# S1 x T1 of the down projection as seven half-size products, and the second block's attention in another order

## The chip, the cores and the metric

The kernel runs on one core of a Trainium2 chip. The metric is the device time in microseconds (us) of one execution. PE is TensorE, DVE is VectorE, ACT is ScalarE, POOL is GpSimd and SP is SyncE; PEld is PE's loading of weights.

## The reference

```python
# S = 2048 tokens, D = 1024, F = 3584, 32 heads of 32, window W = 8, dilation 2
xn = layernorm(x)
q, k, v = split(xn @ wqkv)
logits[s, w] = q[s] . k[s - 2 w] * scale      # -1e9 where s - 2 w < 0
s = (softmax(logits) weighted sum of v[s - 2 w]) @ wo
h = silu(xn @ w1) * (xn @ w3)
g = silu(h @ w2)
out = x + s * g
```

## The kernel before

The tokens are worked in two blocks of 1024 (`b` is 0 or 1), each of two chunks of 512 (chunks 0 to 3; c0 is the even one of a block). Every large product is a 2 x 2 product of halves, done as seven half products with sums of operands before and sums of results after (Strassen's method in Winograd's form). A block goes through these stages on PE: q, k and v (`qkv_pairs`), in block 1 then the output projection of chunk 1 (`wo`), fourteen steps of gate and up projection (`up_step`), the down projection (`mlp_down`), and `wo` of the even chunk. `wo` of chunk 3 comes last.

`mlp_down` multiplies the hidden rows h (2 row halves x 2 halves of F) with w2 (2 halves of F x 2 halves of D). Its seven products run in the order: `w(0,0)`, `w(1,0)`, S2 x T2, S1 x T1, S4 x `w(1,1)`, S3 x T3, h x T4. Each has four row groups `g` of 128 tokens, and each group 14 matmuls of 512 columns on one bank of PSUM. T1 to T4 are sums of w2 that the program keeps in `t_dram`. The S are written by DVE; S1 lies where the tokens' transposed x or its sums were (`s1v`). In the product S1 x T1 the bank `pe[g]` is filled, ACT copies it to SBUF (`dsp`), and S4 x `w(1,1)` goes on adding to the same bank, after which DVE adds (`dsb`). The product S3 x T3 ends in a DVE addition `dsa`, and T4 goes on adding to that bank.

`attention(c)` runs on DVE: the scores (`qk`, `qa`, `qb`, `qc` into the tile E), an exchange over partitions by 16 DMAs (L), the softmax (`z`, `tr`, `zd`, `exp`, `rec`, `pb`), 16 DMAs back into E, and the weighted sum of v (`pv`, `pa`) into `qo`. q, k and v of later chunks wait in DRAM (`park`, `put`, `get`); kT and vT hold one chunk.

The order on every queue is fixed when the program is built. PE runs in the order of the program. The other engines and the DMA queues SP and POOL run in the order that a planner (`Plan`) finds: it lays out all operations with costs of its own and takes, of those ready, the one with the earliest due time, which follows from PE's plan. `plan.soon` shifts due times by name, `plan.chains` fixes the order of named operations, and a `mark` on an operation is a cell that others can wait for. `r8` is a pool of six 8 KB buffers for weights and rows, `k2` one of eight 2 KB buffers, `mm` the eight banks of PSUM. `ln_turn` issues a DMA transpose from ACT's queue. The shared helpers have one line each: `mm` 322, `tt` 331, `cp` 336, `mm_half` 347, `silu` 353, `dma` 359, `ln_turn` 523.

Of the kernel before, what the change touches and what calls it, by code (L numbers as in the profile page):

```python
# [209 lines left out]
def kernel(  # L210
# [489 lines left out]
    def attention(c):  # L700
        u = c % 2
        J4 = [range(0, 4), range(4, 8)]
        r4 = lambda s: s.ap().rearrange("p (j n) -> p j n", j=4)
        if ("q", c) in park:
            get(c, "q")
        if ("k", c) in park:
            halo("k")
            get(c, "k", [("E", W - 1, 3, NR - 1)] if c % 2 else [])
        for w in range(W):
            o = HALO - DIL * w  # L710
            pr = []
# [11 lines left out]
            tt(f"qc{c}", add, lambda w=w: E[:, :, w, :], lambda p0=p0: r4(p0)[:, 0].rearrange("p (q n) -> p q n", n=P),  # L723
               lambda p0=p0: r4(p0)[:, 1].rearrange("p (q n) -> p q n", n=P),
               [p0], [("E", w, sq, r) for sq in range(4) for r in range(NR)], 512, True)
        if ("v", c) in park:
            halo("v")
            get(c, "v")
        L = [plan.slot("att", f"L{c}_{i}") for i in range(2)]
        Lv = lambda i: L[i].ap().rearrange("p (r w n) -> p r w n", r=2, w=W)  # L730
        for r in range(NR):
            for sq in range(4):
                dma((POOL, SP)[sq % 2], f"L{c}", lambda r=r, sq=sq: Lv(r // 2)[sq * 32:(sq + 1) * 32, r % 2],
                    lambda r=r, sq=sq: E[r:P:NR, sq], [("E", w, sq, r) for w in range(W)], [(L[r // 2], r % 2, sq)], 117)
        zf = lambda s: s.ap().bitcast(FP32)
        z = plan.slot("att", f"z{c}")
        zv = lambda: zf(z).rearrange("p (w n) -> p w n", w=W)
        LC = [[(L[i], r, sq) for sq in range(4)] for i in range(2) for r in range(2)]
        tt(f"z{c}", add, zv, lambda: Lv(0)[:, 0], lambda: Lv(0)[:, 1], LC[0] + LC[1], [z], 1024, False)
        tt(f"z{c}", add, zv, zv, lambda: Lv(1)[:, 0], LC[2] + [z], [z], 1024, False)  # L740
        tt(f"z{c}", add, zv, zv, lambda: Lv(1)[:, 1], LC[3] + [z], [z], 1024, False)
        if c == 0:
            tt(f"z{c}", add, lambda: zv()[:, :, 0:HALO], lambda: zv()[:, :, 0:HALO], lambda: maskb[:], [z], [z], 128, False)
        zm = plan.slot("att", f"zm{c}")
        zt = lambda s: zf(s)[:, 0:512].rearrange("p (w n) -> p w n", w=4)

        def tree(t, op):
            tt(f"tr{c}", op, lambda: zt(t), lambda: zv()[:, 0:4], lambda: zv()[:, 4:8], [z], [t], 512, False)
            tt(f"tr{c}", op, lambda: zt(t)[:, 0:2], lambda: zt(t)[:, 0:2], lambda: zt(t)[:, 2:4], [t], [t], 256, False)
            tt(f"tr{c}", op, lambda: zt(t)[:, 0:1], lambda: zt(t)[:, 0:1], lambda: zt(t)[:, 1:2], [t], [t], 128, False)  # L750

        tree(zm, mx)
        tt(f"zd{c}", sub, zv, zv, lambda: zt(zm)[:, 0:1].to_broadcast([P, W, P]), [z, zm], [z], 1024, False)
        plan.op(ACT, f"exp{c}", lambda: nc.scalar.activation(out=zf(z), in_=zf(z), func=ACTF.Exp, scale=scale),  # L754
                [z], [z], 1.07, 0.11, table="exp")
        zs = plan.slot("att", f"zs{c}")
        tree(zs, add)
        plan.op(DVE, f"rec{c}", lambda: nc.vector.reciprocal(out=zt(zs)[:, 0], in_=zt(zs)[:, 0]), [zs], [zs], 0.87)
        pb = plan.slot("att", f"pb{c}")
        pbv = lambda: pb.ap()[:, 0:1024].rearrange("p (w n) -> p w n", w=W)  # L760
        tt(f"pb{c}", mul, pbv, zv, lambda: zt(zs)[:, 0:1].to_broadcast([P, W, P]), [z, zs], [pb], 1024, False)
        for r in range(NR):
            for sq in range(4):
                dma((POOL, SP)[sq % 2], f"E{c}", lambda r=r, sq=sq: E[r:P:NR, sq],
                    lambda sq=sq: pbv()[sq * 32:(sq + 1) * 32], [pb], [("E", w, sq, r) for w in range(W)], 117)
        for jh in range(2):
            js = slice(jh * 4, jh * 4 + 4)
            A = lambda js=js: qo[:, u, js, :]
            Ac = qo_cells(u, J4[jh])

            def pv(dst, wr, w, jh=jh, js=js):
                o = HALO - DIL * w
                q4 = lambda a: a.rearrange("p j (q n) -> p j q n", n=P)
                tt(f"pv{c}", mul, lambda: q4(dst()), lambda: E[:, :, w, :].unsqueeze(1).to_broadcast([P, 4, NST, P]),
                   lambda: q4(vT[:, js, o:o + CH]),
                   [("E", w, sq, r) for sq in range(4) for r in range(NR)] + [("v", j) for j in J4[jh]]
                   + ([("v", j, "halo") for j in J4[jh]] if w else []), wr, 2048, True)
# [170 lines left out]
    def mlp_down(b):  # L948
# [5 lines left out]
        def rhs_load(kind, fh=0, dh=0, t=0):  # L954
            res = []
            for q in range(FH // NQ):
# [3 lines left out]
                if kind == "t":  # L960
                    dma(SP, "t2", v, lambda q=q: t_dram[:, q * NQ:(q + 1) * NQ, t, :],
                        [("td", i) for i in range(q * NQ, (q + 1) * NQ)], [wt], 896)
# [33 lines left out]

        hb = lambda fh, row, g: (lambda: h_sb[:, F_[fh], gs[row][g]])
# [19 lines left out]
        for g in G:  # L1017
            tt("s1", add, lambda g=g: s1v(g), fit(g, hb(0, 1, g)), fit(g, hb(1, 1, g)), hcl(0, 1, g) + hcl(1, 1, g), s1_cells(g), NS, True)
            tt("s3", sub, hf(0, 1, g), hb(0, 0, g), hb(0, 1, g), hcl(0, 0, g) + hcl(0, 1, g), hcl(0, 1, g), NS, True)
        for g in G:  # L1020
            pb.append(bank(f"db{b}_{g}"))
            cp("dfork", pb[g].ap, pa[g].ap, [pa[g]], [pb[g]])
            tt("s2", sub, fit(g, hf(0, 0, g)), lambda g=g: s1v(g), fit(g, hb(0, 0, g)), s1_cells(g) + hcl(0, 0, g), hcl(0, 0, g), NS, True)
# [10 lines left out]
        for g in G:  # L1034
# [3 lines left out]
        rhs = rhs_load("t", t=T1)  # L1038
        pe, sp5 = [], []
        for g in G:  # L1040
            pe.append(bank(f"de{b}_{g}"))
            for q, (wt, ops) in enumerate(rhs):
                mm(pe[g], [lambda g=g, k=k: s1_k(g, k) for k in range(q * NQ, (q + 1) * NQ)], ops, q == 0,
                   [wt] + s1_cells(g), last=q == 1, mark=[("pr", 12 + g)])
            if b + 1 < NB and g == 0:
                ln_turn(2 * b + 3, 0, xn[1], ("pr", 12))
                ln_turn(2 * b + 3, 1, xn[1], ("pr", 12))
            if b + 1 < NB and g == 3:
                ln_turn(2 * b + 3, 2, xn[1], ("pr", 15))
                ln_turn(2 * b + 3, 3, xn[1], ("pr", 15))  # L1050
# [37 lines left out]
    def wo_load():  # L1088

        wots = []  # L1090
        for dh in range(2):
            wot = plan.slot("r8", f"wo{dh}")
            dma(SP, "wo", lambda wot=wot: wot.ap().rearrange("p (j n) -> p j n", j=NJ),
# [184 lines left out]
    plan.chains.append("qs5q0 qs5q1 qforkq0 qforkq1".split())  # L1278
    for st in range(NST):
# [20 lines left out]
    for b in range(NB):  # L1300
# [24 lines left out]
        else:  # L1325
            attention(c0 - 1)
# [18 lines left out]
        def first(b=b):  # L1345
            if b:
                w1o.extend(wo_load())
# [50 lines left out]
```

## Time and profile before

| | |
|---|---|
| median of 3 runs | 717.15 us (717.07 to 718.08) |
| profiled execution, span from first to last instruction | 715.3 us |
| the median less that span | 1.8 us |
| PE busy | 707.4 us |
| DVE busy | 643.8 us |
| ACT busy | 382.3 us |
| granted clock of PE | 1.000 |

The profile is one execution of its own; for it the span is given, and what lies around the span in a run is read as the difference to the median. Times within the profile count from the span's start. A line of the timeline or of a group names the start, the duration, the engine, the line of the program, the operation, what it writes and reads, and how many there were. Matmuls are pipelined, so the time from start to start is what one costs. Some records of matmuls are missing: a step of twice the usual length is such a one.

### The profile page before, as it was taken

Reading aid. Unit: us, or ns where it says so; the run is one execution under the profiler, and the core shown is the slowest. Engines: PE = TensorE matmul, PEld = TensorE weight load, DVE = VectorE, ACT = ScalarE, POOL = GpSimd, SP = SyncE. Lnnn points to the kernel's source line nnn. Section 1 sums busy time; section 2 is a strip of 40 time slices with the busy share of each in tenths; the row PEclk is TensorE's granted clock in tenths of the full one; section 3 lists DMA queues with packets and bytes.
Section 4 is the critical chain, followed back from the end, with each engine's and each line's share of the span. In section 5 each row is a group of like instructions: output and inputs, shape, how many; then the busy total and the mean of one; then the engine's idle time right before and its main releaser. Section 6 shows DMA issues by size and latency. Waiting matters only on the chain.

```text
span 715.3 us, 9199 instructions
## 1 busy us (share of the span) xinstructions
PE 707.4 (99%) x3287; PEld 343.0 (48%) x3342; DVE 643.8 (90%) x866; ACT 382.3 (53%) x650; POOL 50.7 (7%) x103
## 2 busy tenths in 40 slices
PE   9999999999999999999999999999999999999998
PEld 5555544444444444444555554444444444444443
DVE  7999999997999999599999999676999995899936
ACT  7644556575656799142545354676565654411133
POOL 1020100202000000202000000211000002200000
PEclk9999999999999999999999999999999999999999
DMA  9999966659644758994553569787537347655502
GB/s 331 290 358 345 350 224 203 222 155 300 207 148 169 258 181 237 212 269 125 174 170 131 180 198 337 261 283 244 173 129 239 114 153 213 214 191 177 177 21 97
DMA packets 132205, 151.34 MB, mean 212 GB/s; under 512 B 17216, under 2 KB 109248, under 8 KB 127808
## 3 DMA queue, kind: packets, MB, share of 16 engines
q1 hardware_dynamic: 117168, 121.98, 53.4%
q0 software_dynamic: 6112, 26.22, 10.2%
q10 hardware_dynamic: 8880, 2.56, 1.8%
q8 instruction: 26, 0.43, 0.2%
q14 instruction: 19, 0.16, 0.1%
HBM read 106.96 MB, written 32.51 MB: 195 GB/s over the span
## 4 chain that ended last, share of the span: by engine, by line
PE 99%; issue 0%; DVE 0%; ACT 0%; DVEq 0%
PE mm L322 97%; PE mm L307 1%; PE mm L501 0%; DVE xT L331 0%; ACT xT L508 0%; DVE r L435 0%; PE mm L347 0%; DVE k L305 0%; ACT small L424 0%; DVEq L1393 0%; DVE small L426 0%; DVE eps_t L290 0%; DVE eps_d L291 0%; DVEq L331 0%
## 5 line engine op out<-in xcount | busy, mean ns | idle before, releaser
L322 PEld LDWEIGHTS <-r 128*128 128x128 f16 (+1 forms) x2276 | 240.0, 107 | 244.5 <-DMA r<-in_A_wqkv_dram 0.5
L322 PE MATMUL mm<-xs,r 128*128 128x512 f16 x1280 | 295.2, 379 | 0.0
L322 PE MATMUL mm<-xT,r 128*128 128x512 bf16 (+2 forms) x956 | 224.3, 371 | 2.1
L336 ACT COPY k<-mm 128x512 f32<-128x512 f32 x192 | 112.4, 586 | 93.5 <-PE mm L322 93.0
L322 PE MATMUL mm<-r,h_sb 128*128 128x512 bf16 (+1 forms) x694 | 153.0, 379 | 0.5
L322 PEld LDWEIGHTS <-h_sb 128*128 128x128 f16 (+1 forms) x800 | 78.3, 98 | 94.4
L336 ACT COPY mm<-mm 128x512 f32<-128x512 f32 (+1 forms) x89 | 50.6, 571 | 72.2 <-PE mm L322 68.2
L331 DVE TENSOR_TENSOR a<-a,a 128x2048 bf16<-128x2048 bf16 (+1 forms) x72 | 87.7, 1218 | 0.3
L331 DVE TENSOR_TENSOR a<-qo,kT 128x2048 bf16<-128x2048 bf16 x64 | 77.4, 1219 | 1.4 <-ACT kT L336 1.3
L331 DVE TENSOR_TENSOR a<-E,vT 128x2048 bf16<-128x2048 bf16 x56 | 66.4, 1217 | 0.0
L331 DVE TENSOR_TENSOR k<-mm,k 128x512 f32<-128x512 f32 x72 | 48.1, 684 | 19.9 <-PE mm L322 19.8
L331 DVE TENSOR_TENSOR h_sb<-mm,k 128x512 bf16<-128x512 f32 x96 | 63.0, 684 | 1.0 <-PE mm L322 0.5
L353 ACT ACTIVATE k<-k 128x512 bf16<-128x512 f32 x56 | 34.9, 631 | 45.6 <-DVE k L331 45.6
L331 DVE TENSOR_TENSOR h_sb<-h_sb,k 128x1024 bf16<-128x1024 bf16 x56 | 37.1, 686 | 17.2 <-ACT k L336 17.2
L331 DVE TENSOR_TENSOR r<-r,r 128x1024 f16<-128x1024 f16 (+5 forms) x61 | 49.5, 818 | 0.9 <-DMA xT<-r 0.5
L353 ACT ACTIVATE h_sb<-mm 128x512 bf16<-128x512 f32 x60 | 35.8, 598 | 21.7 <-PE mm L322 21.6
L331 DVE TENSOR_TENSOR a<-a 128x1024 bf16<-128x1024 bf16 (+4 forms) x60 | 37.9, 633 | 6.8 <-ACT a L754 4.4
L336 ACT CAST k<-mm 128x512 bf16<-128x512 f32 x56 | 32.6, 585 | 12.2 <-PE mm L322 12.1
L331 DVE TENSOR_TENSOR qo<-qo,a 128x2048 bf16<-128x2048 bf16 x32 | 38.9, 1216 | 0.0
L359 POOL DMA_DIRECT2D a<-E x32 | 16.7, 528 | 303.6 <-ACT k L336 126.1
L331 DVE TENSOR_TENSOR h_sb<-h_sb 128x512 f16<-128x512 bf16 (+1 forms) x72 | 37.0, 575 | 0.0
L331 DVE TENSOR_TENSOR r<-r 128x1024 f16<-128x1024 bf16 (+1 forms) x34 | 25.7, 780 | 0.0
(98 smaller groups left out, 387.8 us busy)
## 6 DMA issues: line engine op xcount, KB each, us to landing
r<-in_B_w_dram SPq DMA_DIRECT2D x42, 512.0 KB, 4.3
s_dram<-r POOLq DMA_DIRECT2D x14, 1024.0 KB, 5.4
r<-t_dram SPq DMA_DIRECT2D x16, 896.0 KB, 6.1
r<-s_dram SPq DMA_DIRECT2D x14, 1024.0 KB, 4.8
r<-in_B_w_dram SPq DMA_DIRECT2D x12, 896.0 KB, 4.9
r<-in_A_wqkv_dram SPq DMA_DIRECT2D x10, 1024.0 KB, 7.3
h_sb<-in_B_w_dram SPq DMA_DIRECT2D x14, 512.0 KB, 8.9
t_dram<-h_sb POOLq DMA_DIRECT2D x14, 512.0 KB, 6.5
```

Source lines behind the costliest of these rows:

```text
L307: nc.tensor.matmul(plan.pools["mm"][i % 8][:], lhsT=warm[:, 0:P], rhs=warm[:, 0:CH], start=True, stop=True)
L322: nc.tensor.matmul(cut(ps.ap()), lhsT=lhs[k](), rhs=cut(rhs[k]()), start=(first and k == 0), stop=(last and k == n - 1), skip_group_check= ...
L331: plan.op(DVE, name, lambda: fn(out=o(), in0=a(), in1=b()), rd, wr, occ, 0.08, late=late)
L336: plan.op(ACT, name, lambda: nc.scalar.copy(out=o(), in_=a()), rd, wr, occ, 0.11)
L353: plan.op(ACT, name, lambda: nc.scalar.activation(out=o(), in_=a(), func=ACTF.Silu), rd, wr, occ, 0.11, table="silu")
L359: plan.op(eng, name, lambda: e.dma_start(out=o(), in_=a()), rd, wr, occ, 0.0, nbytes=kb * 1024, late=late)
```

## The change

S1 x T1 is done by `product2`. It splits S1 by row groups into two pairs and by F into even and odd hidden rows, and T1 by F in the same way and by columns into halves of 256, and multiplies by the same seven-product method once more: for each of two row groups, seven products of seven matmuls of 256 columns. Four sums of S quarters, four of T quarters and four additions on PSUM are new on DVE, copies of banks on ACT. One `r8` buffer (`ex`) holds two of the sums. T1 is loaded as even and odd rows. The last row group of S2 x T2 is placed behind the first two of the seven products. The transposes of chunk 3 wait for marks in the new product.

`attention` is cut into `scores`, `softmax` and `values`. For chunk 2 the softmax works in rows 20 to 27 of `h_sb`, and the result goes to an `r8` buffer instead of E, so that the scores of chunk 3 can be written to E meanwhile. In block 1 `scores` of chunk 2 stands before the up steps, `softmax` of chunk 2 and `scores` of chunk 3 before step 5, `values` of chunk 2 behind the steps. In block 0 `scores` of chunk 1 stands before `mlp_down`. Due times and one chain on SP are changed.

```diff
@@ attention(c), cut into scores, softmax, values @@
-    def attention(c):
+    def scores(c):
         u = c % 2
-        J4 = [range(0, 4), range(4, 8)]
-        r4 = lambda s: s.ap().rearrange("p (j n) -> p j n", j=4)
         if ("q", c) in park:
             get(c, "q")
         if ("k", c) in park:
             halo("k")
-            get(c, "k", [("E", W - 1, 3, NR - 1)] if c % 2 else [])
+            get(c, "k", [("E", W - 1, 3, NR - 1)] if c == 1 else [("L", 2)])
         for w in range(W):
...
+    def softmax(c):
+        if c != 2:
+            sl = [plan.slot("att", f"sm{c}_{i}") for i in range(3)]
+            L = [lambda i=i: sl[i].ap() for i in range(2)]
+            Lc = [lambda r, sq, i=i: (sl[i], r, sq) for i in range(2)]
+            z, zc = zf(lambda: sl[2].ap()), [sl[2]]
+            zmc, pbc = [sl[0]], [sl[1]]
+            zm, pb = zf(L[0]), lambda: sl[1].ap()[:, 0:1024]
+            Ec = "E"
+        else:
+            hi = plan.slot("r8", f"P{c}")
+            hrow = lambda f, n: h_sb[:, f:f + n, :].rearrange("p f n -> p (f n)")
+            hrc = lambda f, n: [x for k in range(f, f + n) for row in range(2) for x in h_cells([k], row)]
+            L = [lambda i=i: hrow(20 + 2 * i, 2) for i in range(2)]
+            Lc = [lambda r, sq, i=i: ("h", 20 + 2 * i + r, sq // 2, sq % 2) for i in range(2)]
+            z, zc = zf(lambda: hrow(24, 2)), hrc(24, 2)
+            zmc, pbc = hrc(26, 1), hrc(27, 1)
+            zm, pb = zf(lambda: hrow(26, 1)), lambda: hrow(27, 1)
+            Ec = hi
+        PB[c] = (Ec, (lambda: E[:]) if c != 2 else (lambda: hi.ap().rearrange("p (q w n) -> p q w n", q=NST, w=W)))
...
+                    [Lc[r // 2](r % 2, sq)] + [("L", c)] * ((r, sq) == (NR - 1, 3)), 117)
...
+                dma((POOL, SP)[sq % 2], f"E{c}", lambda r=r, sq=sq: P4()[r:P:NR, sq],
+                    lambda sq=sq: pbv()[sq * 32:(sq + 1) * 32], pbc,
+                    [(Ec, w, sq, r) for w in range(W)], 117)
+
+    def values(c):
+        u = c % 2
+        Ec, P4 = PB[c]
...
@@ mlp_down(b) @@
+                    fs = slice(q, FH, 2) if t == T1 else slice(q * NQ, (q + 1) * NQ)
+                    dma(SP, f"t2_{b}{t}{q}", v, lambda fs=fs: t_dram[:, fs, t, :],
+                        [("td", i) for i in range(FH)[fs]], [wt, (wt, 0), (wt, 1)], 896)
...
+        def product2(pe, rhs):
+            ex = plan.slot("r8", "ex")
+            HC = CH // 2
+            I = range(2)
+            w = [wt for wt, _ in rhs]
+            wv = lambda kk, n: (lambda: r8v(w[kk], FP16)[:, 0:NQ * CH].rearrange("p (k n) -> p k n", k=NQ)[:, :, n * HC:(n + 1) * HC])
+            tv = lambda: r8v(ex, FP16)[:, 0:NQ * HC].rearrange("p (k n) -> p k n", k=NQ)
+            uv = lambda: r8v(ex, FP16)[:, NQ * HC:2 * NQ * HC].rearrange("p (k n) -> p k n", k=NQ)
+            part = lambda m, kk, i: [("s1 part", 2 * m + i, kk)]
+            if b + 1 == NB:
+                rows = [((lambda m, kk: (lambda: s1_q2(m, kk))), uv, lambda m, kk: part(m, kk, 0) + part(m, kk, 1),
+                         [(ex, 1), (ex, 2)], 2 * NQ * P)]
+            else:
+                rows = [((lambda m, kk, i=i: (lambda: s1_q(2 * m + i, kk))), (lambda i=i: uv()[:, :, i * P:(i + 1) * P]),
+                         (lambda m, kk, i=i: part(m, kk, i)), [(ex, 1 + i)], NQ * P) for i in I]
+            def in_place(x, y, neg, n):
+                for r, (a, u, cells, uc, size) in enumerate(rows):
+                    dst, src = a(*x), u if y is None else a(*y)
+                    ry = uc if y is None else cells(*y)
+                    pair = (src, dst) if neg else (dst, src)
+                    tt(n, sub, dst, pair[0], pair[1], cells(*x) + ry, cells(*x), size, True)
+            for a, u, cells, uc, size in rows:
+                tt("l2s1", add, u, a(1, 0), a(1, 1), cells(1, 0) + cells(1, 1), uc, size, True)
+            in_place((1, 0), (0, 0), True, "l2s3")
+            tt("l2t1", sub, tv, wv(0, 1), wv(0, 0), [(w[0], 1), (w[0], 0)], [(ex, 0)], NQ * HC, True)
+            tt("l2t3", sub, wv(0, 1), wv(1, 1), wv(0, 1), [(w[1], 1), (w[0], 1)], [(w[0], 1)], NQ * HC, True)
+            lhs = lambda m, kk, i: ([lambda k=k: s1_q(2 * m + i, kk)[:, k, :] for k in range(NQ)],
+                                    part(m, kk, i) + s1_cells(2 * m + i))
+            lhu = lambda i: ([lambda k=k: uv()[:, k, i * P:(i + 1) * P] for k in range(NQ)], [(ex, 1 + i)])
+            rw = lambda kk, n: ([lambda k=k: wv(kk, n)()[:, k, :] for k in range(NQ)], [(w[kk], n), w[kk]])
+            rt = ([lambda k=k: tv()[:, k, :] for k in range(NQ)], [(ex, 0)])
+            def p(ps, n, A, B, first=False, mark=()):
+                a, ra = A
+                c, rc = B
+                def emit():
+                    for k in range(NQ):
+                        nc.tensor.matmul(half(ps.ap, n)(), lhsT=a[k](), rhs=c[k](), start=first and k == 0, stop=k == NQ - 1,
+                                         skip_group_check=True)
+                plan.op(PE, "mm2 " + ps.name, emit, ra + rc, [ps] + list(mark), NQ * 0.1092, 0.0)
+            for i in I:
+                p(pe[2 + i], 0, lhs(0, 0, i), rw(0, 0), True)
+            for i in I:
+                p(pe[2 + i], 1, lhu(i), rt)
+            in_place((0, 0), None, True, "l2s2")
+            tt("l2t2", sub, wv(0, 0), wv(1, 1), tv, [(w[1], 1), (ex, 0), (w[0], 0)], [(w[0], 0)], NQ * HC, True)
+            s15 = []
+            for i in I:
+                s15.append(plan.slot("k2", "l2s15"))
+                cp("l2s15", lambda i=i: f32(s15[i]), pe[2 + i].ap, [pe[2 + i]], [s15[i]])
+                cp("l2fork", half(pe[i].ap, 0), lambda i=i: f32(s15[i])[:, 0:HC], [s15[i]], [pe[i]], 0.33)
+            yield
+            for i in I:
+                p(pe[i], 0, lhs(0, 1, i), rw(1, 0))
+                p(pe[2 + i], 0, lhs(0, 0, i), rw(0, 0), mark=[("pr", 12)] * i)
+                cp("l2u2", half(pe[i].ap, 1), half(pe[2 + i].ap, 0), [pe[2 + i]], [pe[i]], 0.27)
+            in_place((0, 1), (0, 0), False, "l2s4")
+            tt("l2t4", sub, wv(1, 0), wv(1, 0), wv(0, 0), [(w[1], 0), (w[0], 0)], [(w[1], 0)], NQ * HC, True)
+            for i in I:
+                p(pe[2 + i], 0, lhs(1, 0, i), rw(0, 1))
+                tt("l2c22", add, half(pe[2 + i].ap, 1), half(pe[2 + i].ap, 0), lambda i=i: f32(s15[i])[:, HC:CH],
+                   [pe[2 + i], s15[i]], [pe[2 + i]], HC, False)
+            for i in I:
+                p(pe[i], 1, lhs(0, 1, i), rw(1, 1))
+                tt("l2c12", add, half(pe[i].ap, 1), half(pe[i].ap, 1), lambda i=i: f32(s15[i])[:, HC:CH],
+                   [pe[i], s15[i]], [pe[i]], HC, False)
+            for i in I:
+                p(pe[2 + i], 0, lhs(1, 1, i), rw(1, 0), mark=[("pr", 15)] * i)
...
+        def t2(g):
             prod(pb[g], g, 0, 0, rhs, False, FP16, [("pr", 8 + g)])
             su2.append(plan.slot("k2", "dsu"))
             cp("dsu", lambda g=g: f32(su2[g]), pb[g].ap, [pb[g]], [su2[g]])
-        rhs = rhs_load("t", t=T1)
+        for g in G[:-1]:
+            t2(g)
+        rhs1 = rhs_load("t", t=T1)
         pe, sp5 = [], []
         for g in G:
             pe.append(bank(f"de{b}_{g}"))
-            for q, (wt, ops) in enumerate(rhs):
-                mm(pe[g], [lambda g=g, k=k: s1_k(g, k) for k in range(q * NQ, (q + 1) * NQ)], ops, q == 0,
-                   [wt] + s1_cells(g), last=q == 1, mark=[("pr", 12 + g)])
-            if b + 1 < NB and g == 0:
-                ln_turn(2 * b + 3, 0, xn[1], ("pr", 12))
-                ln_turn(2 * b + 3, 1, xn[1], ("pr", 12))
-            if b + 1 < NB and g == 3:
-                ln_turn(2 * b + 3, 2, xn[1], ("pr", 15))
-                ln_turn(2 * b + 3, 3, xn[1], ("pr", 15))
+        steps = product2(pe, rhs1)
+        next(steps)
+        t2(NST - 1)
+        for _ in steps:
+            pass
+        if b + 1 < NB:
+            for g in G:
+                ln_turn(2 * b + 3, g, xn[1], ("pr", 12 if g < 2 else 15))
+        for g in G:
             sp5.append(plan.slot("k2", "dsp"))
             cp("dsp", lambda g=g: f32(sp5[g]), pe[g].ap, [pe[g]], [sp5[g]])
...
@@ order of the whole @@
+    plan.chains.append("t2_021 wo0_0".split())
...
-            attention(c0 - 1)
+            softmax(c0 - 1)
+            values(c0 - 1)
...
+        if b:
+            scores(c0)
         for fb in range(FB):
+            if b and fb == 5:
+                softmax(c0)
+                scores(c1)
             up_step(b, fb)
-        attention(c0)
+        if not b:
+            scores(c0)
+            softmax(c0)
+        values(c0)
+        if not b:
+            scores(c1)
         t4_last = mlp_down(b)
-        wots = wo_load()
+        wots = wo_load(b)
         wo_sums(wots)
         wo(c0, wots)
-    attention(3)
+    softmax(3)
+    values(3)
     wo(3, wots, last=t4_last)
     flush()
-    plan.soon = {n + c: -200.0 for c in "03" for n in ("L", "z", "tr", "zd", "exp", "rec", "pb", "E")}
+    plan.soon = {n + c: -200.0 for c in "013" for n in ("L", "z", "tr", "zd", "exp", "rec", "pb", "E")}
+    plan.soon.update({n + c: d for c, d in (("2", 50.0), ("3", 0.0)) for n in ("qk", "qa", "qb", "qc")})
     plan.run()
```

More of the change, by code (lines that the diff above doesn't have):

```diff
@@ L697, in qkv_pairs, with r4 @@
             pend.append(tail)
-    def attention(c):
+    J4 = [range(0, 4), range(4, 8)]
+    def r4(s):
+        return s.ap().rearrange("p (j n) -> p j n", j=4)
+    PB = {}
+    def scores(c):
         u = c % 2
-        J4 = [range(0, 4), range(4, 8)]
-        r4 = lambda s: s.ap().rearrange("p (j n) -> p j n", j=4)
         if ("q", c) in park:
@@ L728, in attention @@
             get(c, "v")
[L729 to L765, printed above, removed]
         for jh in range(2):
@@ L773, in pv @@
                 q4 = lambda a: a.rearrange("p j (q n) -> p j q n", n=P)
[L774 removed]
+                tt(f"pv{c}", mul, lambda: q4(dst()), lambda: P4()[:, :, w, :].unsqueeze(1).to_broadcast([P, 4, NST, P]),
                    lambda: q4(vT[:, js, o:o + CH]),
[L776 removed]
+                   [(Ec, w, sq, r) for sq in range(4) for r in range(NR)] + [("v", j) for j in J4[jh]]
                    + ([("v", j, "halo") for j in J4[jh]] if w else []), wr, 2048, True)
@@ L995, in fit, with s1_q, s1_q2, s1_parts @@
             return (lambda: a().rearrange("p (k s) n -> p k s n", s=2)) if b + 1 < NB and g == 3 else a
+        def s1_q(g, kk):
+            if b + 1 < NB and g == 3:
+                return s1v(g)[:, :, kk, :]
+            return s1v(g)[:, kk:FH:2, :]
+        def s1_q2(m, kk):
+            return xT16[:, m].rearrange("p k n -> p (k n)")[:, 0:FH * 256].rearrange("p (f n) -> p f n", f=FH)[:, kk:FH:2, :]
+        def s1_parts(g):
+            return [("s1 part", g, kk) for kk in range(2)]
+        def product2(pe, rhs):
[65 more added lines that the diff above has]
+                p(pe[2 + i], 0, lhs(1, 1, i), rw(1, 0), mark=[("pr", 15)] * i)
```

42 lines of the change are left out of this document (34 added, 8 removed).

## The prediction

> **What bounds the kernel now.** I read the page first, then PE's own waits.
>
> ```profile
> span 715.3 us, 9199 instructions
> PE 707.4 (99%) x3287; PEld 343.0 (48%) x3342; DVE 643.8 (90%) x866; ACT 382.3 (53%) x650; POOL 50.7 (7%) x103
> PE 99%; issue 0%; DVE 0%; ACT 0%; DVEq 0%
> ```
> ```profile
> PE mm L307 <- DVE k L305: 1.2, 1, 1.2
> PE mm L501 <- DVE r L435: 0.2, 1, 0.2
> ```
> PE waits twice, 1.4 us in all, both in the first 9 us. After that every start of a 512-wide matmul follows the last by 0.216 us until 711.6; the few steps of 0.43 us are one missing record each. So the end is a sum of matmuls, and no other engine's work is in it: the change can gain only what it takes off PE, and can lose only by making PE wait where it never waited.
>
> Next the timeline around S1 x T1, and of the only long runs of half-width matmuls there are:
>
> ```profile
> 288.61 9.23 PE L322 MATMUL mm<-r,xs 128*128 128x512 f16 x42
> 300.70 36.42 PE L322 MATMUL mm<-r,h_sb 128*128 128x512 bf16 x166
> ```
> ```profile
> 710.59 0.97 PEld L347 LDWEIGHTS <-qo 128*128 128x128 bf16 x8
> 710.80 1.04 PE L347 MATMUL mm<-h_sb,qo 128*128 128x256 f16 x8
> ```
> S1 x T1 of block 0 runs from 288.61 to 300.70, 12.09 us: 4 row groups x 14 matmuls x 0.2159 (9.23 less the last one's 0.38, over 41 steps). Eight 256-wide matmuls, each with its own weight load, start at 710.804 to 711.568: 0.109 us apart.
>
> Last, where DVE has room (columns: PE, PEld, DVE, ACT, POOL):
>
> ```profile
> 280.00:300.00 20.00, 20.00 (x94) 9.09 (x93) 15.21 (x21) 8.64 (x13) 4.18 (x8) 1.00 0.97 249
> 300.00:320.00 20.00, 19.89 (x92) 9.07 (x93) 14.40 (x18) 7.61 (x10) 0.00 (x0) 1.00 0.96 246
> ...
> 460.00:480.00 20.00, 19.89 (x92) 9.07 (x93) 13.70 (x21) 14.88 (x24) 0.00 (x0) 1.00 0.90 303
> 480.00:500.00 20.00, 19.95 (x94) 9.08 (x93) 12.90 (x17) 11.95 (x21) 4.22 (x8) 1.00 0.76 225
> ...
> 680.00:700.00 20.00, 19.89 (x92) 9.02 (x93) 8.65 (x16) 8.96 (x16) 0.00 (x0) 1.00 0.09 31
> ```
> DVE's idle stretches are the softmaxes (they wait for the exchanges E to L and back) and the end.
>
> **PE, the sum.** A block's product becomes 7 products x 2 row pairs x 7 matmuls = 98 of 256 columns: 98 x 0.109 = 10.68 us, against 12.09: 1.41 us less, twice, 2.8 us. With a step of 0.108 or 0.110 it is 3.0 or 2.6. Break-even is a step of 12.09 / 98 = 0.123 us. The weight load takes 0.098 (any operand stored in rows of 128), so 0.011 is left in each step; the 256-wide run at 12.02 us steps by 0.109 even with loads of 0.143.
> The Trainium skill, page "TensorE: Matmul & The Clock Gate", section "Back-to-back issue gap", speaks against this: it says that in a stream of weight load and matmul the spacing is set by both, and gives 81 ns sustained for 128 columns and 131 ns for 512, so (an estimate, on a straight line between) about 98 ns for 256. By it the block's product would go from 7.3 to 9.6 us and the change would lose some 4.5 us. The trace disagrees at 512 (0.216) and for narrow ones (transposes of 128 columns start 0.056 apart).
>
> **DVE, added.** Block 0: eight sums of S quarters (896 elements; between 0.42 for 512 and 0.69 for 1024: 0.62) 4.9 us, four of T halves (1792: 1.08) 4.3, four 256-wide PSUM adds (0.42) 1.7: 10.9 us. Block 1 takes S in four of 1792: 4.3 + 4.3 + 1.7 = 10.3. Together 21 us on an engine with 71 us idle. Block 0: T1 landed at 280.4 and 284.0, the first half product starts at 288.61 - 3.02 = 285.6 (one group of T2 now comes after it), so sums begin near 281. They push scores(1), which ended at 295.3, to about 306; behind it lay 10.4 us of idle time up to 320 and the deadline of chunk 1 (wo(1), after 430). Priced at nothing on this cover; without it, below.
> **ACT, added.** Per block two full copies (0.59) and four half ones (0.36): 2.6 us where ACT is busy 8.6 of 20. Nothing.
>
> **New waits of PE.** All are inside the product, on one bank handed PE -> ACT or DVE -> PE. ACT starts 0.31 us after the start of a bank's last matmul. (a) l2u2: half copy 0.36, then some 0.05 to wake PE: 0.72; PE fills this with the 7 matmuls of the other row pair, 0.76 + 0.11. Margin 0.15, cost nothing. (b) c12 and then dsp of bank 0: 0.31 + 0.42 + 0.04 + 0.59 + 0.05 = 1.4; three products, 2.4, cover it. A 2048-wide DVE operation (1.22) just begun ahead of c12 makes 2.6: 0.2 lost. (c) c22, S4 and T4 before the fifth to seventh products: about 2 us of DVE work in 2.3 to 3 us; 0 to 0.5 lost. I take 0.1 per block for (b) and (c), high end 0.7.
> (d) Block 0 only: the transposes of chunk 3 are issued on ACT's queue behind pr 12 and pr 15, and pr 12 now lies in the middle of the product. In the trace two in a row hold that queue for:
>
> ```profile
> 291.89 3.52 ACTq L523 DMA_TRANSPOSE xT<-r  x2
> 300.96 5.02 ACTq L523 DMA_TRANSPOSE xT<-r  x2
> ```
> Queued behind them is dsp of bank 0, for which w(1,1)'s first product waits. Counted from the last matmul at pr 12 the pair starts at 0.35; dsp must start by 4.05. A pair of 2.7 (1.35 each at 271.8) or 3.52 costs nothing, one of 5.02 costs 1.3. I take 0.2, ends 0 and 1.3.
>
> **Buffers and queues.** "ex" takes the buffer of x2, into which the first half of w(1,1) went at 281.48. That half now follows T2's buffers: issued near 290 and 291.5, landing 4.6 to 6.6 later (the two landings before), 298 at worst, needed at 299.1 and 300.6. Nothing; if a load beside it stretches it to 9.7 (the t_dram load of 301.21), 0.6. T1's interleaved rows are the same bytes in the same 1 KB pieces. On SP, wo's load is held behind T4's second half (issued at 313.74); it has landed 6.1 to 7.9 after its issue, so by 323, and is needed at 336.96: nothing. On DVE, softmax(1) gets rank over the dsa sums, which the T4 products wait for: z to zd is some 6 us in a row, the first dsa is ready near 314.5 and due at 323: nothing, at worst 0.5.
> Block 1: scores(2) and (3) cost the same instructions as before, softmax(2) the same 32 DMAs on SP and POOL, now with L, z and p in h_sb rows 20 to 27 and the copy of P in one r8 buffer until values(2) ends. Up steps keep 5 buffers for 2.5 steps of loads that land in 4.3 to 4.8 us of a 12.09 us step: nothing. T2 of block 1 is the load likely to inherit that buffer, some 24 us into the stage. K and q of chunk 3 are fetched behind the last L DMA (9.2 us): scores(3) starts some 18 us after scores(2) ends, and then fills the hole of 460 to 500 and, with values(2), that of 580 to 620 (13.4 and 9.7 us idle). I count 15 of these 23 as recovered; on the time that is worth nothing directly, as PE does not wait there.
>
> **Sum.** 715.3 - 2.8 + 2 x 0.1 + 0.2 = 712.9 for the span. The runs' median lies 1.8 above the profiled span (717.15 to 715.3); I keep that: 714.7. What 0.2% (1.4 us) is: about the least that a measurement of this kernel tells from no change.
>
> **Rivals.** *The hand-offs eat it* (same): pair of transposes 1.3, late w(1,1) 0.6, (b) and (c) 0.7 in one block: 717.15 - 2.8 + 2.6 = 717.0. For: the margins of 0.15 to 1 us; against: ACT and DVE have short queues there. 0.13.
> *DVE becomes the bound* (slower): the 21 us do not disappear into holes, since a softmax waits for DMAs whatever DVE has to do, and shift attention(3) to the end. There DVE idles 11.35 of the last 20 us before 700 and 1.3 in those before: 12.7. From a backlog of 12.7 us on, wo(3) waits; all 21.2 make 8.5: 717.15 - 2.8 + 8.5 = 722.9. For: DVE is full from 620 to 660. Against: the overlap of scores(3) with softmax(2), and idle time in block 0. 0.12.
> *Half-width matmuls don't cost half* (slower): weight load and stream in series, 0.098 + 0.107 = 0.205, give 20.1 us a block: 717.15 + 16 = 733. It decides above 0.123. Against: the eight at 710.8. 0.02. A milder form: the loads alone pace the stream, at 0.143, the longest in the run at 12.02 us: 14.0 us a block, 721.0; that run itself speaks against it. 0.01. (The Trainium skill's spacing, above, is of this form.)
> *Not seven* (same): the loops give p called 2+2+2+2+2+2+2 times a block, 14 x 7 = 98. 0.01, 717.2.
>
> **Numbers.** The main case has 0.71. Faster by over 0.2%: 0.71; within: 0.13 + 0.01, and 0.01 of a small backlog, 0.15; slower 0.14. Range: 713.9 (a step of 0.108 and no wait, less the runs' own 0.2) to 717.2, which takes in the first rival and leaves out about 0.17.
>
> **What would show it.** Right: 98 matmuls of 256 columns per block starting 0.109 apart, S1 x T1 taking 10.7 us; PE's waits in the product under 0.5 us a block; DVE busier in 460 to 500 and 580 to 620, idle time before 700 no less than now. Wrong: a PE wait on ACT behind DMA_TRANSPOSE, on w(1,1)'s load, or on DVE after 684 (wo(2), wo(3)); or starts 0.12 apart.

## The result, and the profile after

The changed kernel takes 720.19 us (median of 7 runs, 719.37 to 723.67) against 717.33 (7 runs, 717.05 to 718.08) before: a ratio of 1.0051, 95% interval 1.0032 to 1.0070, slower by 2.9 us by the medians and 3.7 by the ratio. The profiled execution is the fastest of its runs, 719.37 us with a span of 717.6; three of the seven lie at 722.8 to 723.7, and no profile shows what they lose beyond it.

The page of after, then PE's waits (what waited, for what: us in total, times, longest):

```profile
span 717.6 us, 9471 instructions
PE 708.5 (99%) x3426; PEld 351.0 (49%) x3426; DVE 661.5 (92%) x894; ACT 386.2 (54%) x662; POOL 50.6 (7%) x103
PE 95%; DMA 2%; DVE 1%; ACTq 1%; issue 0%; ACT 0%; DVEq 0%
```
```profile
PE mm L322 <- ACT k L336: 2.4, 1, 2.4
PE mm L307 <- DVE k L305: 1.3, 1, 1.3
PE mm L501 <- DVE r L435: 1.2, 2, 0.9
PE mm L322 <- DVE r L331: 0.5, 1, 0.5
PE mm L322 <- DMA r<-in_B_w_dram: 0.2, 1, 0.2
```

The chain was 99% PE before; now ACT's queue, DVE and a load of weights stand in it. Three lines of waits are new behind the first 9 us. The third line, at the start, is no loss here: PE reaches the matmul that began at 21.11 us before at 20.96.

The chain that ended last (start, us, what) goes through the new product and out of it:

```profile
285.59 3.06 PE mm L1083 x28
288.65 3.02 PE mm L322 x14
291.67 3.07 PE mm L1083 x28
294.76 0.36 ACT mm L336
295.12 1.02 ACTq L523
296.18 4.88 ACTq L523
301.10 0.59 ACT k L336
301.74 46.65 PE mm L322 x208
```

L1083 is the new product: 28 matmuls in 3.06 us, 0.109 each, as forecast. Then the chain leaves PE. A small copy on ACT is followed by the two transposes issued behind pr 12, and the next copy, `dsp` of bank 0, starts only at 301.10. The timeline of ACT and PE says the same (in brackets, idle time before the line and what ended it):

```profile
294.77 6.29 ACTq L523 DMA_TRANSPOSE xT<-r  x2
301.10 0.58 ACT L336 COPY k<-mm 128x512 f32<-128x512 f32 x1 [5.98 <-DVE a L331]
301.74 6.47 PE L322 MATMUL mm<-r,h_sb 128*128 128x512 bf16 x22 [2.42 <-ACT k L336]
```

The copy's own input is ready, its releaser is an old one, and the 5.98 us are the queue's. The pair holds the queue 6.29 us, where pairs of 3.52 and 5.02 had been seen before. The 22 matmuls behind it take 6.47 us and not 22 x 0.216 = 4.75: of the first eight steps six are of 0.427 us, twice the usual one, and the first and the last, of 0.38 and 0.35, lie between. The stretches show it as a granted clock (columns as before: us, then PE, PEld, DVE, ACT, POOL, then the clock, the DMA share and GB/s):

```profile
300.00:320.00 20.00, 18.27 (x78) 8.02 (x78) 11.03 (x16) 4.66 (x9) 4.16 (x8) 0.91 1.11 228
...
480.00:500.00 20.00, 20.00 (x95) 9.07 (x93) 17.74 (x25) 14.18 (x23) 1.71 (x4) 1.00 0.71 246
580.00:600.00 20.00, 20.00 (x94) 9.11 (x93) 17.43 (x21) 12.40 (x22) 4.16 (x8) 1.00 0.69 221
...
680.00:700.00 20.00, 20.00 (x94) 9.11 (x93) 16.55 (x23) 7.29 (x13) 0.00 (x0) 1.00 0.11 37
```

From PE's starts the account closes. Two products: -2.8. At 299.04 a step of 2.70 us, 2.59 over the 0.109 of a half-width matmul, and eight slow steps of 3.29 us in all, 1.56 over eight normal ones: +4.1 (the expectations below have 4.2). At 351.45, in block 1's first product with wqkv, which waits for a sum on DVE: +0.6. At 605.7, in `w(0,0)` of block 1, whose second half was issued at 594.84 and landed 11.4 us later beside the fetch of v: +0.4. With the start's -0.15 that is +2.2, and the spans differ by 717.6 - 715.3 = 2.3.

SP's queue shows what had moved. Of after:

```profile
290.19 1.75 SPq L359 DMA_DIRECT2D r<-in_B_w_dram  x2
291.99 7.71 SPq L359 DMA_DIRECT2D r<-t_dram  x3
...
316.84 0.60 SPq L359 DMA_DIRECT2D r<-t_dram  x1
```

And of before:

```profile
281.48 6.18 SPq L359 DMA_DIRECT2D r<-in_B_w_dram  x2
...
313.74 0.76 SPq L359 DMA_DIRECT2D r<-t_dram  x1
```

`w(1,1)` (the in_B_w_dram pair) is issued at 290.19 and 291.56 instead of 281.48 and 287.29, and now shares 290 to 302 with T3's two halves, T4's first half and the transposes. By the trace's landing times the pair's transposes took 9.9 and 14.9 us, against 4.6 and 4.4 before.

### The profile page after: what moved, and what is told of

It reads as the page before. It is cut to its first block, busy times and chain, and to the rows that moved or that the text cites. A ratio compares the mean times of both kernels' runs of the same rounds, so it can differ in the third digit from the quotient of the medians.

```text
span 717.6 us, 9471 instructions
## 1 busy us (share of the span) xinstructions
PE 708.5 (99%) x3426; PEld 351.0 (49%) x3426; DVE 661.5 (92%) x894; ACT 386.2 (54%) x662; POOL 50.6 (7%) x103
## 4 chain that ended last, share of the span: by engine, by line
PE 95%; DMA 2%; DVE 1%; ACTq 1%; issue 0%; ACT 0%; DVEq 0%
PE mm L322 92%; PE mm L1083 2%; DMA r<-in_B_w_dram 2%; ACTq L523 1%; DVE small L419 0%; DVE r L331 0%; DMA r<-in_A_x_dram 0%; PE mm L501 0%; DVE r L435 0%; DVE xT L331 0%; ACT k L336 0%; PE mm L347 0%; DVE small L422 0%; ACT mm L336 0%; DVEq L1531 0%
## 5 line engine op out<-in xcount | busy, mean ns | idle before, releaser
L322 PE MATMUL mm<-xT,r 128*128 128x512 bf16 (+1 forms) x996 | 227.1, 372 | 0.0
L336 ACT COPY k<-mm 128x512 f32<-128x512 f32 x196 | 114.2, 586 | 87.7 <-PE mm L322 74.7
L322 PE MATMUL mm<-r,h_sb 128*128 128x512 bf16 (+1 forms) x704 | 155.8, 382 | 2.6 <-ACT k L336 2.4
L331 DVE TENSOR_TENSOR a<-a,a 128x2048 bf16<-128x2048 bf16 (+1 forms) x68 | 84.0, 1235 | 1.1 <-DMA a<-E 0.9
L331 DVE TENSOR_TENSOR r<-r,r 128x1024 f16<-128x1024 bf16 (+5 forms) x67 | 57.0, 859 | 1.1 <-DMA xT<-r 0.5
L331 DVE TENSOR_TENSOR a<-E,vT 128x2048 bf16<-128x2048 bf16 x42 | 50.1, 1227 | 0.0
L331 DVE TENSOR_TENSOR h_sb<-h_sb 128x512 f16<-128x512 bf16 (+5 forms) x83 | 46.4, 618 | 3.8 <-DMA h_sb<-E 2.5
L331 DVE TENSOR_TENSOR a<-a 128x1024 bf16<-128x1024 bf16 (+4 forms) x53 | 34.7, 658 | 1.0 <-DMA a<-E 0.8
L331 DVE TENSOR_TENSOR r<-r 128x1024 f16<-128x1024 bf16 (+2 forms) x36 | 28.4, 820 | 0.0
L359 POOL DMA_DIRECT2D a<-E x24 | 12.5, 525 | 175.1 <-DVE qo L331 89.1
```

The costliest lines, as they stand in the source:

```text
L322: nc.tensor.matmul(cut(ps.ap()), lhsT=lhs[k](), rhs=cut(rhs[k]()), start=(first and k == 0), stop=(last and k == n - 1), skip_group_check= ...
L331: plan.op(DVE, name, lambda: fn(out=o(), in0=a(), in1=b()), rd, wr, occ, 0.08, late=late)
L336: plan.op(ACT, name, lambda: nc.scalar.copy(out=o(), in_=a()), rd, wr, occ, 0.11)
L359: plan.op(eng, name, lambda: e.dma_start(out=o(), in_=a()), rd, wr, occ, 0.0, nbytes=kb * 1024, late=late)
```

## The experiments

Theory A: the 4.1 us at 299 come from the pair of transposes on ACT's queue ahead of `dsp`. Rivals: the transposes' late landing costs as much elsewhere (DVE, SP and x3's buffer wait for it); the attention's new order costs the time; the product itself does. Ratios are against the kernel before, with 95% intervals. A mark only tells the planner when to queue a DMA; on the chip the order of the queue and the data decide.

### The place of the transposes, moved back

**turns_last**: all four transposes behind the product.
```diff
-                ln_turn(2 * b + 3, g, xn[1], ("pr", 12 if g < 2 else 15))
+                ln_turn(2 * b + 3, g, xn[1], ("pr", 15))
```


> The changed kernel with the first two transposes of chunk 3 waiting for the end of the new product (pr 15) like the other two; nothing else differs, on any queue but ACT's. Theory (ACT's queue): the second transpose held ACT for 4.88 us, the copy dsp of bank 0 came 2.5 us late, and PE then ran 8 steps at 0.427 in place of 0.216. Expect no PE wait at the end of block 0's product (under 0.3 us), no step of 0.427 after the first 9 us, and 720.2 - 4.2 = 716.0 us, some 715.3 to 716.3. Rival (the hand-offs of the product itself, c12 and DVE): PE waits there as before, 2 us and more, and the time stays at 719 to 720. Rival (load of w(1,1), landed at 298.60 against a need at 299.1): the wait moves to that load and stays at 1 us or more.

Measured: 720.70 us (718.12 to 722.05), 1.0043 [1.0028, 1.0057]; the profiled run is the slowest, 722.05. PE's waits:

```profile
PE mm L322 <- DVE k L331: 2.5, 1, 2.5
PE mm L322 <- DMA r<-t_dram: 2.4, 1, 2.4
...
PE mm L322 <- ACT k L336: 0.3, 1, 0.3
```

The wait at 299 and the slow steps are gone, so A names that wait rightly. But two waits of the same size stand in the T4 product. SP and DVE in that stretch:

```profile
309.99 11.90 SPq L359 DMA_DIRECT2D a<-E  x5
...
322.71 0.60 SPq L359 DMA_DIRECT2D r<-t_dram  x1
```
```profile
321.48 2.36 DVE L331 TENSOR_TENSOR xs<-xT 128x2048 f16<-128x2048 bf16 x2 [8.51 <-DMA a<-E]
```

Five DMAs of the exchange spread over 11.9 us on SP: four of them go out at 309.99, 313.58, 319.31 and 321.42, each just as a transpose has landed (309.97, 313.56, 319.29, 321.40). SP's own waits put 11.6 us in this stretch down to these four landings. By the trace's semaphore records (116, 118, 107 and 109) each of the four DMAs waits for the semaphore that tells of that transpose's landing, and tells of its own landing by the same one: the queues are tied by a reused semaphore, and the transfers share no data (E to a, r to xT). No run took that tie away. T4's second half follows at 322.71 and lands at 330.84. On DVE the sum of x's transposes heads the queue until the last has landed, and `dsa`, which T4's product waits for, is behind it. (The line names the exchange as releaser; the start is that of the last landing.) So here the late landing costs PE about as much as the held queue did. But it is later than in after, 321.40 and not 315.54, because the move itself put it there. In after the first `dsa` had ended at 321.48 and T4's second half had landed at 325.37; PE came for them at 327.5 and 329.0, and without the 4.1 us would have come near 323.4 and 324.9 (an estimate). So after hid some 0.5 us of such a wait, and the rest is new.

**one_turn_mid**: one transpose behind pr 12, three behind pr 15.
```diff
-                ln_turn(2 * b + 3, g, xn[1], ("pr", 12 if g < 2 else 15))
+                ln_turn(2 * b + 3, g, xn[1], ("pr", 12 if g < 1 else 15))
```


> The changed kernel with one transpose behind pr 12 and three behind pr 15. Theory, that only the second of a pair is held: the single one takes 1.4 us of ACT's queue, dsp of bank 0 is on time, and the time is that of the kernel with all four at the end, 715.3 to 716.3. Rival (any transpose here is held, since loads are in flight): the single one is held 4 to 5 us, PE waits 1 to 2.5 us and the time is 717.5 to 720.

Measured: 722.95 (721.02 to 723.79), 1.0070 [1.0058, 1.0083]. Nothing at 299; 2.5 us for T4's second half and 1.6 for DVE's `dsa` instead, then eight steps of 0.427, then steps of 1.17 and 1.26 at 354 and 609. A single transpose amid the product (it held 1.92 us) does not hurt there, and three behind it (2.15, and 10.47 for two) do. The forecast of 715.3 to 716.3 missed here as it did for turns_last.

### The two halves of the change alone

**order_only**: the new attention order, S1 x T1 as before.
```diff
-        steps = product2(pe, rhs1)
...
+            for q, (wt, ops) in enumerate(rhs):
+                mm(pe[g], [lambda g=g, k=k: s1_k(g, k) for k in range(q * NQ, (q + 1) * NQ)], ops, q == 0,
+                   [wt] + s1_cells(g), last=q == 1, mark=[("pr", 12 + g)])
```


> The new order of attention alone, with S1 x T1 as four groups of 14 full matmuls as before. Theory: PE is the bound, so nothing is gained; what is lost is only what the new order puts into PE's way at the start of block 1's q product (0.6 us) and at its first down product (0.4 us): 717.3 to 718.4, no PE wait near 300. Rival (the new order is what costs): 719 and more.

Measured: 718.18 (717.59 to 719.31), 1.0013 [1.0004, 1.0021]. One wait behind the start, at 602.5:

```profile
PE mm L322 <- DMA r<-in_B_w_dram: 1.6, 1, 1.6
```

The order alone costs some 0.9 us by the medians. In the profiled run, the slowest of its eleven, the second half of block 1's `w(0,0)` is issued only at 599.13, behind an exchange DMA that goes out at 598.57 as v's fetch lands (598.55); it lands 5.3 us later, at 604.43. PE waits for nothing from 290 to 320.

**product_only**: `product2` with the old `attention`.
```diff
-    def scores(c):
+    def attention(c):
...
-            get(c, "k", [("E", W - 1, 3, NR - 1)] if c == 1 else [("L", 2)])
+            get(c, "k", [("E", W - 1, 3, NR - 1)] if c % 2 else [])
```


> The seven half-size products alone, with attention and its order as before. Theory (ACT's queue): the wait near 300 is there as in the changed kernel, 2 to 2.7 us and slow steps behind it, and block 1 gains its 1.4: 717.3 - 2.8 + 4.2 = 718.7. Rival of the prediction (DVE becomes the bound without the new order): in addition PE waits for DVE from 684 on, up to 8.5 us, so 720 to 727.

Measured: 722.19 (720.86 to 723.51), 1.0065 [1.0053, 1.0077]. PE waits 2.3 us for ACT at 299 behind a pair of 6.21 us, the slow steps follow, 0.6 at 352, and some 0.7 us for DVE between 695 and 702. The median lies 1.3 above this run, the lowest of five, and 3.5 above the theory's 718.7; where the other runs lose that, no profile shows. So the loss at 299 belongs to the product's side of the change, and without the new order DVE is late at the end.

**block1_only**: the product in block 1 only, the new order, and a chain on SP that puts `w(0,0)` ahead of v's fetch (its loads get names of their own for that). In block 0, S1 x T1 stands as in the kernel before.
```diff
-                    fs = slice(q, FH, 2) if t == T1 else slice(q * NQ, (q + 1) * NQ)
+                    fs = slice(q, FH, 2) if t == T1 and b else slice(q * NQ, (q + 1) * NQ)
...
-                    dma(SP, "w2", v, lambda f=f: w2_r[:, f:f + NQ, dh * CH:(dh + 1) * CH], [], [wt], 896)
+                    dma(SP, f"w2_{b}{fh}{dh}{q}", v, lambda f=f: w2_r[:, f:f + NQ, dh * CH:(dh + 1) * CH], [], [wt], 896)
...
+    plan.chains.append("w2_1001 getv3".split())
```


> The seven half-size products in block 1 alone, block 0 with the 56 full matmuls and its transposes as before; new order of attention, and the fetch of v for chunk 3 chained behind the second half of w(0,0). Theory (all of the loss is block 0's transposes and what waits for them): one block's 1.4 us gained and no PE wait over 0.3 us after the first 9 us: 715.7 to 716.3. Rival (the new order costs 0.9 as it did alone): 716.8.

Measured: 716.13 (715.83 to 716.90), 0.9982 [0.9973, 0.9990]. PE waits for nothing after the start. Where the product has no transposes behind it, it brings 1.3 us of the 1.4 computed. Its pairs of transposes, back at their old place, hold 3.61 and 5.20 us.

### The transposes placed ahead of the traffic

**turns_early**: the first two behind the third group of S2 x T2.
```diff
-                ln_turn(2 * b + 3, g, xn[1], ("pr", 12 if g < 2 else 15))
+                ln_turn(2 * b + 3, g, xn[1], ("pr", 10 if g < 2 else 15))
```


> The changed kernel with the first two transposes of chunk 3 behind pr 10 (the third group of S2 x T2, some 9 us earlier, when no weight load is in flight) and the last two behind pr 15 as in the change. Theory: a transpose holds ACT's queue, lands late and holds back what waits for it (the x sums on DVE, T4's second half on SP) when it meets loads in flight. So the early pair takes some 2.7 us of ACT's queue and lands within 6 us, PE doesn't wait near 299, the late pair lands by 312, T4's products don't wait, and the time is 715.2 to 716.3. Rival (any two transposes behind pr 15 meet the L exchange and land past 318): PE waits 2 to 5 us near 324, 718 to 720.

Measured: 718.38 (716.59 to 720.15), 1.0009 [0.9999, 1.0019]. The early pair holds 1.25 and 2.83 us and has landed by 289; T4's second half goes out at 310.60. PE waits neither at 299 nor at 324, and yet the median is 2 us above the theory's range. The profiled run's largest wait is left in the next stage, for a sum of wqkv at 347, late in DVE's order behind other work:

```profile
PE mm L322 <- DVE r L331: 2.3, 1, 2.3
```

**t3_loads_late**: T3's loads made to wait, in the plan, for pr 15.
```diff
-                        [("td", i) for i in range(FH)[fs]], [wt, (wt, 0), (wt, 1)], 896)
+                        [("td", i) for i in range(FH)[fs]] + [("pr", 15)] * (b == 0 and t == T3), [wt, (wt, 0), (wt, 1)], 896)
```


> The changed kernel with T3's loads of block 0 issued only behind pr 15, so that the first pair of transposes meets the loads of w(1,1) alone. Theory (loads in flight hold the second transpose): the pair takes 2.7 to 3.6 us in place of 6.3 and PE's wait near 299 is under 0.5 us. Rival (the second transpose is held by the first alone, whatever else moves): 6 us and a wait of 2 us or more. The time may still hold a wait for T4, 716 to 720.

Measured: 722.68 (720.00 to 724.11), 1.0067 [1.0050, 1.0084]. The loads did not move: issued at 291.94 and 296.24, against 291.99 and 296.29. It is a repeat of after (pair 6.09 us, PE waits 2.2 for ACT) and decides nothing about T3's part in the hold.

**best_1**: turns_early, with the transposes written behind the `w(1,1)` products, so that T4's second half takes `w(1,1)`'s buffer and not x3's, and with the chain of block1_only.
```diff
-        if b + 1 < NB:
-            for g in G:
-                ln_turn(2 * b + 3, g, xn[1], ("pr", 10 if g < 2 else 15))
...
+        if b + 1 < NB:
+            for g in G:
+                ln_turn(2 * b + 3, g, xn[1], ("pr", 10 if g < 2 else 15))
...
+    plan.chains.append("w2_1001 getv3".split())
```


> turns_early with two more edits: the transposes are written into the program behind the products of w(1,1), so that T4's second half takes a buffer of w(1,1) and not that of x3, which waits for the transposes; and the fetch of v for chunk 3 is chained behind the second half of w(0,0) in block 1. Theory: no wait near 299 or 324, none at block 1's first down product; what is left is the start of block 1's q product, 0.6 us: 714.6 to 715.4. Rival (the order of attention costs in itself): 716.5 or more.

Measured: 714.52 (714.46 to 715.00), 0.9959 [0.9947, 0.9971]: 2.8 us faster than before, 5.7 faster than after. All of PE's waits:

```profile
PE mm L307 <- DVE k L305: 1.3, 1, 1.3
PE mm L501 <- DVE r L435: 0.3, 1, 0.3
```
and the transposes on ACT's queue:
```profile
285.85 3.32 ACTq L523 DMA_TRANSPOSE xT<-r  x2
...
299.59 1.25 ACTq L523 DMA_TRANSPOSE xT<-r  x1
...
300.88 4.16 ACTq L523 DMA_TRANSPOSE xT<-r  x1
```

PE waits only at the start again, and the sum of matmuls sets the end. The product is the same as in after; only when DMAs are issued differs.

### Which part of best_1 does it

Four kernels, each best_1 with one thing taken back.

**best_pair_mid**: the pair back at pr 12.
```diff
-                ln_turn(2 * b + 3, g, xn[1], ("pr", 10 if g < 2 else 15))
+                ln_turn(2 * b + 3, g, xn[1], ("pr", 12 if g < 2 else 15))
```


> best_1 with the first two transposes put back behind pr 12, in the middle of the product; T4's second half stays out of x3's buffer. Theory (ACT's queue): the wait near 299 is back, 2 to 2.7 us, and behind it some eight steps at 0.427, 1.7 us: 714.5 + 4.2 = 718.7, from 717.5 to 719.5. Rival (what best_1 mended was T4's buffer alone): 714.5 to 715.3.

Measured: 720.95 (718.89 to 727.90), 1.0049 [1.0032, 1.0066]. The profiled run is the slowest, so its waits are an upper case:

```profile
PE mm L322 <- DVE k L331: 3.5, 1, 3.5
PE mm L322 <- DMA r<-in_A_wqkv_dram: 3.4, 3, 2.0
PE mm L322 <- ACT k L336: 2.2, 1, 2.2
```
```profile
296.31 6.04 ACTq L523 DMA_TRANSPOSE xT<-r  x2
```

One mark moved, and 6.4 us are lost. The pair holds 6.04 us, the transposes land after 10.0 to 18.7 us, the last at 325.51, and the waits for ACT and for `dsa` (the DVE line) come back. T4's second half, its free buffer notwithstanding, goes out at 326.09, behind the exchange.

**best_all_last**: all four behind pr 15.
```diff
-                ln_turn(2 * b + 3, g, xn[1], ("pr", 10 if g < 2 else 15))
+                ln_turn(2 * b + 3, g, xn[1], ("pr", 15))
```


> best_1 with all four transposes behind pr 15; T4's second half in a buffer of w(1,1). Theory: nothing near 299 and T4's load on time, but the four transposes run beside the loads and the L exchange, land near 320, the x sums wait for them at the head of DVE's queue, and dsa behind these: a wait of 1 to 2.5 us in T4's products, 715.5 to 717.5. Rival (it was the buffer alone that made T4 wait): 714.5 to 715.0.

Measured: 720.08 (717.06 to 724.87), 1.0038 [1.0017, 1.0060].

```profile
PE mm L322 <- DMA r<-in_A_wqkv_dram: 2.7, 3, 1.8
PE mm L322 <- DVE r L331: 2.0, 1, 2.0
```
```profile
301.19 10.98 ACTq L523 DMA_TRANSPOSE xT<-r  x3
```

The 299 wait is away, and the wait for `dsa` is 0.6 us, less than forecast; PE's large waits are for `wqkv`, some 25 us later, and the time is above the forecast range. T4's second half has a free buffer, and still goes out at 319.96, behind SP's exchange DMAs and just after the last landing at 319.38: its buffer was not the only thing that held it.

**best_no_v_chain**: without the chain.
```diff
-    plan.chains.append("w2_1001 getv3".split())
```


> best_1 without the chain that puts the fetch of v for chunk 3 behind the second half of w(0,0). Theory: the fetch and the L exchange share the DMA engines with that load, PE waits 0.4 to 0.9 us for it near 603: 714.9 to 715.5. Rival (the load is in time without the chain once block 0 is mended): 714.5.

Measured: 714.94 (714.43 to 716.47), 0.9968 [0.9956, 0.9980]. The profiled run (714.43) has no wait at 603. The chain is not needed for the gain; one run of five, 716.47, is outside best_1's spread, and no profile says why.

**best_old_order**: with the old `attention` and its order (the diff of product_only).


> best_1 with attention and its order as in the kernel before (one function, softmax of chunk 2 in its own tiles and E, due times as before). Theory (the new order is what makes room on DVE for the product's 21 us): PE waits for DVE from 684 on, 0.9 us as with the product alone or up to some 3 us: 715.3 to 717.5. Rival (DVE has room either way): 714.5.

Measured: 716.34 (716.22 to 716.89), 0.9987 [0.9978, 0.9996]. In the profiled run PE waits 0.5 us for a sum of `wqkv` at 348 and loses 0.7 between 691 and 698 on DVE; another 0.5 lies behind PE's last matmul, and the span is 1.9 longer than best_1's. The new order is worth some 1.8 of the 2.8 us (716.34 - 714.52, with the kernel before at 717.34 and 717.40 beside them).

## Why the prediction was wrong

**The sum on PE held.** In block 1 the new product runs from 639.92 to 653.64 with one 3.02 us group of T2 within: 10.70 us, for 10.68 forecast. The step is 0.109 in block 0 too. The Trainium skill's spacing (page "TensorE: Matmul & The Clock Gate", section "Back-to-back issue gap"), by which 256 columns would cost an estimated 98 ns, is not what the trace shows. Rivals three and four, that half width does not cost half or that there are not seven, fell.

**(a), (b), (c) held, below their price.** Of the 0.1 us a block for hand-offs, PE shows none within the product in after.

**(d) is the step that failed.** It priced the transposes at 0.2, 1.3 at most, from pairs that had held the queue 2.7, 3.52 and 5.02 us. It named the mechanism (`dsp` of bank 0 behind the pair on ACT's queue) and the sign to look for, and mis-sized it: the pair held 6.29 us. By (d)'s own sum 3.70 us of that are free (4.05 - 0.35), and the other 2.59 are what the step at 299.04 lost. No term held the eight matmuls that ran at up to twice their time behind the wait, 1.56 more and 4.1 in all. The durations were taken from traffic that the change itself replaced: with the old product a pair held 3.78 us (order_only, at 291.95), with the new one 6.21 (product_only).

**"Buffers and queues" failed with it.** The paragraph moved `w(1,1)` to 290 and 291.5 correctly (290.19 and 291.56) and asked only if it lands in time; it did, at 295.3 and 298.6. It did not carry the move over to (d): those loads now lie beside the transposes. Nor did it follow a late landing of the transposes to who waits for it: DVE's x sums at the head of the queue, SP's exchange, and T4's second half (316.84 instead of 313.74), priced at nothing. turns_last, where the last lands 5.9 us later than in after, shows 5 us there. The remaining two terms, 0.6 in q's product and 0.4 at block 1's `w(0,0)`, were priced at nothing as well.

**The rivals.** "The hand-offs eat it" had the right line of the profile and ended within 0.2% of the time before, where the ratio is 1.0051. "DVE becomes the bound" did not occur: PE waits for nothing from 640 on in after. But my count was too good. In all DVE's busy time grew by 17.7 us (661.5 - 643.8), where I had 21. It grew by 4.8 us in 480 to 500 and 3.1 in 580 to 600, with 0.2 each in their neighbours, some 8.3 of the 15 that I counted as recovered, and before 700 it has 3.45 us idle of 20, no longer 11.35. best_old_order and product_only put PE's loss to DVE at the end at about 0.7 us without the new order; the rival's 8.5 needed all 21 us to reach the end.

**The forecast's number as a kernel.** best_1, with the same product and the same order of attention, runs at 714.52; 714.7 was forecast. Its span of 712.8 stands beside the sum's 712.9: the prediction computed the kernel as it is without the DMA collisions. That the two agree to 0.1 us is in part luck: the 0.4 us of waits in the sum are not there, and some 0.2 us are lost elsewhere, at 347.

**Still open.** Why the second transpose holds the queue is only seen as a gradient, from 282 us on: a first one holds 1.25 to 1.95 us, one behind it 1.27 when the load in flight had landed (best_1 at 287.89; T1's second half landed at 286.95) and 2.2 to 6.1 with loads in flight (the longest in one_turn_mid). In the trace of before two holds end 0.13 and 0.28 us ahead of the landing of the load in flight (295.42 and 295.55; 305.98 and 306.26), which fits a queue that drains. In after the long hold ends at 301.06, 1.26 us ahead of the next landing of a load (302.32), which doesn't, and no experiment separated T3's load from the others. Nor is it shown why runs of after, turns_last, best_pair_mid and best_all_last spread over 4 to 9 us and those of best_1 over 0.5. Part of it goes with the clock: in turns_early the five runs up to 717.39 have a granted clock of 0.999 or 1.000 and the six from 718.38 on one of 0.997, and best_all_last divides in the same way between 719.76 and 720.08.

## What to carry to other kernels

Price a DMA that a change moves by the traffic at its new place, counting the loads that the same change moves there, and follow its landing to every queue whose head waits for it. A DMA moved out of the way of one wait may land late and make another as long at its new place, so take a wait away on the chip before crediting its whole length. An extra buffer is a moved load: find which transfer inherits the buffer that it took.

## What the runs showed of the hardware

**A transpose on the issuing queue.** One DMA transpose of 128 rows (0.26 MB by the packets of the queue) holds ACT's queue 1.25 us or more, and work for ACT's own engine behind it waits. In best_1 the early pair landed 3.2 and 3.1 us after its issues; in after, beside 896 KB loads, transposes took 9.9 to 14.9 us, in best_pair_mid up to 18.7. The Trainium skill, page "Advanced Engine Details and Errata", section "X-Bar Transpose (TRN2)", says that these transposes are as fast as ordinary DMAs. The trace disagrees beside other traffic: 0.26 MB in 14.9 us, where the 896 KB halves of `w(1,1)` took 5.2 and 7.0 and those of T3 10.3 and 11.8.

**The clock after an idle stretch.** PE idle for 2.4 us at 299 is followed by 8 steps of up to 0.427 instead of 0.216, 3.3 us in all; idle for 0.5 us (at 351) is not. In turns_last two stretches of 2.5 and 2.4 us left no slow step, nor did one of 3.5 us in best_pair_mid (for `dsa`), and in one_turn_mid the second of 1.6 and 2.5 us did. The Trainium skill, page "TensorE: Matmul & The Clock Gate", section "Part 1: The HAM clock gate", has the clock fall after an idle window of about 3.4 us and rise after a busy one of the same length. The slow stretch of 3.3 us agrees; the fall came here after a shorter idle time, and not each time.
